# Top-k attention with a capacity-limited mixture of experts: a new order of VectorE's work inside a pipeline step, and one copy for q and k

## The chip, the cores and the metric

The kernel runs on one core of a Trainium2 chip. The metric is the device time of one execution in microseconds (us), the median of several runs. The core has five engines that matter here: TensorE (PE in the profile), VectorE (DVE), ScalarE (ACT), GpSimd (POOL) and SyncE (SP), which issues the DMA transfers. Matrix products land in PSUM, everything else is worked on in SBUF.

## The reference, cut to what matters

Attention over 8 batches, 8 heads, 576 tokens and a head size of 64. Of every row of 576 scores only the 32 largest are kept. A mixture-of-experts layer follows, with one expert for each token and at most 80 tokens for each expert.

```python
def _attn_ref(q, k, v):
    B, H, S, D = q.shape                                  # 8, 8, 576, 64
    top_k = 32
    scores = scale * np.matmul(q, k.transpose(0, 1, 3, 2))
    kth = np.partition(scores, -top_k, axis=-1)[..., -top_k:-top_k + 1]
    mask = scores >= kth
    scores = np.where(mask, scores, -1000000000.0)
    scores = scores - np.max(scores, axis=-1, keepdims=True)
    attn = np.exp(scores)
    attn = attn / (np.sum(attn, axis=-1, keepdims=True) + 1e-09)
    return np.matmul(attn, v).astype(np.float32)

# x = attention's result as (4608, 512); for each expert e of 8, at most 80 tokens:
#   out[tok] = gate_w[tok] * (relu(x[tok] @ w1[e]) @ w2[e])
```

The change is in the attention alone.

## The kernel before

The attention is a software pipeline written as a list of engine instructions in a fixed order. Its item of work is a **unit**: 128 rows (queries) of one head with their 576 scores. A pair of heads has nine units, numbered 0 to 8 here: four row blocks with two heads each (0 and 1, 2 and 3, 4 and 5, 6 and 7), and one last unit, 8, that holds the 64 rows left over from both heads. There are 32 head pairs, so 288 units. The second unit of each of the four blocks (1, 3, 5, 7) is in the set `odd`; unit 8 and unit 0 of the next pair are both not in it.

The threshold of a unit is found in these pieces, each of which is one letter in the step's schedule:

```python
def parts(self, i):                       # G: six of these, 96 scores each
    for j in range(NG):
        nc.vector.max(out=cand[:, j, :], in_=s[:, j * S // NG : (j + 1) * S // NG])
        yield

def search(self, i):
    for r in range(3):                    # a, c, e: a maximum over the 48 candidates
        nc.vector.max(out=dst, in_=cand)
        if r == 2:                        # after e: ScalarE compares and counts
            nc.scalar.activation(sign, s, Act.Sign, bias=w9[:, 7:8], scale=-1.0, accum_out=cnt)
        yield
        if r < 2:                         # b, d
            nc.vector.match_replace(out=cand, in_to_replace=dst, in_values=cand, imm_value=LOW)
            yield
    y = self.rows.tile([P, S], F32, name="y", tag="y", bufs=1)
    engine = nc.gpsimd if i in self.odd else nc.vector
    engine.tensor_tensor(out=y, in0=s, in1=sign, op=Alu.mult)      # y: the product
    yield
    nc.vector.max(out=w9[:, 8:], in_=y)                            # g: the search in the product
    yield
    nc.vector.scalar_tensor_tensor(out=pick, in0=past, scalar=cnt, in1=w9[:, 7:],
        accum_out=self.thr[:, i : i + 1], op0=Alu.is_equal, op1=Alu.mult)   # h: the pick
    yield

def below(self, i):                       # m: the mask
    if i in self.odd:
        nc.scalar.activation(self.mask[i], self.s[i], Act.Relu, bias=self.thr[:, i : i + 1], scale=-1.0)
        return
    engine = nc.vector if i == NU - 1 else nc.gpsimd
    engine.tensor_scalar(self.mask[i], self.s[i], self.thr[:, i : i + 1], None, op0=Alu.is_lt)
```

One call of `step(i, ...)` works on several units at once. The letters b to e belong to the unit one behind `i`, y to the unit two behind, g three behind, h and m four behind; G and a belong to `i` itself, and z is a small reciprocal.

```python
back = dict(a=0, b=1, c=1, d=1, e=1, y=2, g=3, h=4, m=4)
for c in "hmgyGbGcGdGGGeaz" if i - 2 in self.odd else "hmgGbGcGdGeGGyaz":
    ...                                   # the letter's next piece, for unit i - back[c]
if whole(i - 4): self.turn_w(...)         # TensorE: scores and mask turned and added, then ScalarE's exponential
...
if busy: self.front(...)                  # TensorE: scores of a later unit; ScalarE copies them out of PSUM
if whole(i - 5): self.back(...)           # TensorE: weights times v
if due and not busy: self.turn(due.pop()) # once for each head pair
```

`turn` turns q and k of the next head pair on TensorE and copies them out of PSUM on ScalarE:

```python
four = self.four()                                        # four PSUM banks
ps = [four[:, 2 * j : 2 * j + 2, :].rearrange("p j c -> p (j c)") for j in range(2)]
for j, src in enumerate(self.qk.pop(n)):
    self.turn_in(ps[j], src.rearrange("p c h d -> p c (h d)"))
self.turned[n] = [self.qkp.tile([P, S], F32, name=name, tag=name) for name in ("qT", "kT")]
for j in range(2):
    nc.scalar.copy(self.turned[n][j], ps[j][:, :S])
```

Each engine takes its instructions in the order in which the loop emits them, so the letters are VectorE's order, and, for y and m of the units that go there, GpSimd's.

Of the kernel before, what the change touches and what calls it, by code (L numbers as in the profile page):

```python
# [9 lines left out]
F32 = mybir.dt.float32  # L10
# [17 lines left out]
def kernel(  # L28
# [11 lines left out]
    nc = tc.nc  # L40
    B, H, S, D = q.shape
# [8 lines left out]
    P = 128  # L50
# [76 lines left out]
    class Attention:  # L127
# [53 lines left out]
        def turn(self, n):  # L181

            four = self.four()
            ps = [four[:, 2 * j : 2 * j + 2, :].rearrange("p j c -> p (j c)") for j in range(2)]
            for j, src in enumerate(self.qk.pop(n)):
                self.turn_in(ps[j], src.rearrange("p c h d -> p c (h d)"))
            self.turned[n] = [self.qkp.tile([P, S], F32, name=name, tag=name) for name in ("qT", "kT")]
            for j in range(2):
                nc.scalar.copy(self.turned[n][j], ps[j][:, :S])

        def front(self, n, t):

# [199 lines left out]
        def run(self, slow):  # L392

            units = []
            for n in range(NP):
                for t in range(NF):
                    units += [(n, t, 0), (n, t, 1)]
                units.append((n, NF, 2))
            self.odd = {i for i, unit in enumerate(units) if unit[2] == 1}
            first, second = {}, {}  # L400
            later = []
            due = []
            drawn = []
            ready = {}

            def whole(i):

                return 0 <= i < NU and units[i][2] > 0

            def step(i, last):  # L410
                if 0 <= i < NU:
                    n, t, h = units[i]
                    if t == 2 and h == 1 and n + 2 < NP:
                        self.load(n + 2, *divmod(n + 2, HP))
                    if t in (1, 3) and h == 0 and slow and n:
                        slow.pop(0)()
                    if t == 0 and h == 0 and n + 1 < NP:
                        due.append(n + 1)
                    first[i] = self.parts(i)

                back = dict(a=0, b=1, c=1, d=1, e=1, y=2, g=3, h=4, m=4)

                for c in "hmgyGbGcGdGGGeaz" if i - 2 in self.odd else "hmgGbGcGdGeGGyaz":
                    if c == "G":
                        if 0 <= i < NU:
                            next(first[i])
                    elif c == "a":
                        if 0 <= i < NU:
                            next(first[i], None)
                            second[i] = self.search(i)  # L430
                            next(second[i])
                    elif c == "z":
                        for u in drawn:
                            self.over(*u)
                    elif c == "m":
                        if 0 <= i - back[c] < NU:
                            self.below(i - back[c])
                    elif i - back[c] in second:
                        next(second[i - back[c]])
                if whole(i - 4):  # L440
                    self.turn_w(*units[i - 4][:2])
                for u in drawn:
                    self.divide(*u)
                ends = [n for n, t in drawn if t == NF]
                drawn.clear()
                busy = 0 <= i + 4 < NU and units[i + 4][2] != 1
                if busy:
                    self.front(*units[i + 4][:2])
                if whole(i - 5):
                    self.back(*units[i - 5][:2])  # L450
                    drawn.append(units[i - 5][:2])
                if due and not busy:
                    self.turn(due.pop())
                    busy = True
                for g in list(later):
                    if ready[g] and busy and not last:
                        continue
                    busy = busy or ready[g] == 1
                    ready[g] = next(g, None)
                    if ready[g] is None:  # L460
                        later.remove(g)
                for n in ends:
                    b, hp = divmod(n, HP)
                    later.append(self.norm(n, b, hp, b % 2, 2))
                    ready[later[-1]] = 0

            with tc.manual_schedule():
                self.load(0, 0, 0)
                self.load(1, *divmod(1, HP))
                nc.sync.dma_start(wg, moe_w_gate.rearrange("(c p) e -> p c e", p=P))  # L470
                self.turn(0)
                i = -4
                while i < NU + 6 or later:
                    step(i, i >= NU + 6)
                    i += 1
            assert not slow and not due
# [410 lines left out]
```

## Time and profile before

The median time is 1022.78 us (three runs, 1022.1 to 1024.26). The profiled execution has a span of 1027.5 us. All 288 units lie in its first 890 us or so; the experts follow.

| line, engine | what it is | count | median or mean ns of one |
|---|---|---|---|
| L213 DVE | G, a maximum over 96 scores | 1728 | 244 |
| L224 DVE | a, c, e | 864 | 199 |
| L232 DVE | b, d (a load and a replace) | 576 | 191 |
| L236 DVE | y on VectorE | 160 | 740 |
| L236 POOL | y on GpSimd | 128 | 1281 |
| L238 DVE | g, the search in the product | 288 | 755 |
| L241 DVE | h, the pick | 288 | 211, mean 290 |
| L254 POOL | m on GpSimd | 159 | 1721 |
| L250 ACT | m on ScalarE | 128 | 777 |
| L229 ACT | sign and count | 288 | 777, and 198 for the count |
| L189 ACT | copies of q and of k | 32 each | 643 and 647 |

How to read it: durations of neighbours on VectorE overlap[...]. What an instruction costs its engine is the distance from its start to the next start, which the timeline shows: 0.16 us for a G of 0.24, 0.67 us for a g of 0.755.

### The profile page before, as it was taken

To read this page: it belongs to the slowest core of one execution; us is meant where nothing else is said; L and a number is where in the kernel's file an instruction comes from. 1 tells how busy PE (TensorE), PEld (TensorE's weight loads), DVE (VectorE), ACT (ScalarE), POOL (GpSimd) and SP (SyncE) were. 2 spreads that over 40 slices of the span, in tenths; PEclk is the share of its full clock that TensorE was granted. 3 is DMA by queue.
4 is the path that set the end of the run, shared out by engine and by line. 5 is a ranking of instruction groups with operands and counts; after the bars stand their busy time and mean duration, and the time that the engine had idled before them with its cause. 6 is when DMAs were issued, how large, how long until landed. Compare 5 with 4: busy or idle time off the path is not lost.

```text
span 1027.5 us, 35579 instructions
## 1 busy us (share of the span) xinstructions
PE 902.3 (88%) x13381; PEld 728.9 (71%) x13381; DVE 896.0 (87%) x5087; ACT 786.2 (77%) x1671; POOL 456.1 (44%) x331
## 2 busy tenths in 40 slices
PE   5889999999889999989899999998999998598896
PEld 3677777777667777777677777776777777588886
DVE  3999999999999999999999999999999999551000
ACT  3888899888888898888898888898888988401110
POOL 1444555554454545554454544555454554211101
PEclk9999999999999999999999999999999999879998
DMA  4344443333333323233333311111221200326800
GB/s 93 77 118 129 122 128 89 89 89 89 90 88 89 80 72 81 77 81 84 85 89 89 89 41 38 46 45 48 48 49 48 49 13 14 119 77 214 325 23 25
DMA packets 167893, 85.76 MB, mean 83 GB/s; under 512 B 117792, under 2 KB 154656, under 8 KB 167712
## 3 DMA queue, kind: packets, MB, share of 16 engines
q1 hardware_dynamic: 166688, 80.78, 28.4%
q0 software_dynamic: 1024, 2.62, 0.8%
q8 instruction: 107, 1.75, 0.7%
q14 instruction: 74, 0.61, 0.2%
HBM read 63.19 MB, written 20.19 MB: 81 GB/s over the span
## 4 chain that ended last, share of the span: by engine, by line
DVE 54%; PE 30%; ACT 11%; issue 2%; another core or an unknown queue 1%; DMA 0%; SPq 0%; POOL 0%; POOLq 0%; ACTq 0%; DVEq 0%
DVE cand L213 17%; DVE w L238 12%; PE cc L309 7%; DVE cand L232 6%; DVE y L236 6%; DVE pick L241 4%; DVE top L224 4%; PE yp L776 3%; PE sp L201 3%; PE ab L286 3%; ACT wT L295 3%; PE sp L178 2%; ACT sign L229 2%; PE warm L632 2%; DVE w L224 2%
## 5 line engine op out<-in xcount | busy, mean ns | idle before, releaser
L213 DVE MAX8 cand<-s 128x8 f32<-128x96 f32 x1728 | 387.0, 244 | 9.5 <-ACT s L206 9.5
L254 POOL TENSOR_SCALAR mask<-s,thr_all 128x576 bf16<-128x576 f32 x159 | 273.7, 1721 | 199.6 <-PE ab L291 130.6
L309 PEld LDWEIGHTS cc<-vb,wT 128*64 128x64 f32 x5760 | 201.2, 139 | 111.5 <-ACT wT L295 94.6
L236 POOL TENSOR_TENSOR y<-s,sign 128x576 f32<-128x576 f32 x128 | 164.0, 1281 | 240.3 <-ACT sign L229 104.2
L309 PE MATMUL cc<-vb,wT 128*64 128x65 f32 x5760 | 223.4, 225 | 52.1 <-ACT wT L295 52.1
L229 ACT ACTIVATE sign<-s,w 128x576 bf16<-128x576 f32 x288 | 226.0, 785 | 44.9 <-DVE w L224 44.5
L238 DVE MAX8 w<-y 128x8 f32<-128x576 f32 x288 | 217.4, 755 | 2.2 <-POOL y L236 2.0
L201 PE MATMUL sp<-kT,qT 64*128 64x288 f32 (+1 forms) x1280 | 202.0, 435 | 14.7 <-ACT part L353 6.1
L286 PE MATMUL ab<-ident,s 128*128 128x128 f32 x1152 | 176.5, 282 | 10.9 <-ACT wT L295 10.9
L206 ACT ACTIVATE s<-sp 128x1152 f32<-128x1152 f32 (+1 forms) x160 | 167.2, 1045 | 11.4 <-PE sp L201 9.8
L286 PEld LDWEIGHTS ab<-ident,s 128*128 128x128 f32 x1152 | 128.3, 142 | 34.6 <-ACT wT L295 25.1
L295 ACT ACTIVATE wT<-ab 128x1024 f32<-128x1024 f32 (+1 forms) x160 | 150.8, 942 | 0.0
L201 PEld LDWEIGHTS sp<-kT,qT 64*128 64x128 f32 (+1 forms) x1280 | 105.5, 179 | 53.4 <-ACT part L353 8.0
L236 DVE TENSOR_TENSOR y<-s,sign 128x576 f32<-128x576 f32 x160 | 118.2, 739 | 3.1 <-ACT sign L229 2.6
L224 DVE MAX8 top<-cand 128x8 f32<-128x48 f32 x576 | 114.4, 199 | 0.1
L291 PEld LDWEIGHTS <-mask 128*128 128x128 bf16 x1440 | 94.5, 98 | 25.8 <-ACT mask L250 19.0
L232 DVE MATCH_REPLACE8 cand<-top,cand 128x48 f32<-128x48 f32 x576 | 110.0, 191 | 0.0
L250 ACT ACTIVATE mask<-s,thr_all 128x576 bf16<-128x576 f32 x128 | 99.5, 777 | 0.4 <-DVE pick L241 0.4
L330 ACT ACTIVATE xn<-cc,z_all 128x64 f32<-128x64 f32 (+1 forms) x320 | 82.8, 316 | 2.3 <-DVE z_all L321 2.3
L241 DVE SCALAR_TENSOR_TENSOR pick<-past,cnt,w 128x9 f32<-128x9 f32 x288 | 83.6, 290 | 0.0
L286 PE MATMUL cc<-ident,s 128*128 128x128 f32 x288 | 79.0, 274 | 0.2 <-ACT xn L330 0.2
L293 ACT ACTIVATE wT<-cc 128x256 f32<-128x256 f32 (+1 forms) x160 | 57.5, 359 | 6.0 <-PE cc L291 4.4
(192 smaller groups left out, 981.5 us busy)
## 6 DMA issues: line engine op xcount, KB each, us to landing
w<-in_moe_w_dram SPq DMA_DIRECT2D x32, 512.0 KB, 4.3
w<-in_moe_w_dram SPq DMA_DIRECT2D x8, 2048.0 KB, 12.6
out_dram<-zero SPq DMA_DIRECT2D x9, 1024.0 KB, 5.9
qn<-in_q_dram SPq DMA_DIRECT2D x64, 128.0 KB, 2.4
kn<-in_k_dram SPq DMA_DIRECT2D x64, 128.0 KB, 2.5
vb<-in_v_dram SPq DMA_DIRECT2D x64, 128.0 KB, 2.5
xd<-xn SPq DMA_DIRECT2D x32, 256.0 KB, 4.1
qn<-in_q_dram SPq DMA_DIRECT2D x32, 32.0 KB, 2.3
```

The costliest lines, as they stand in the source:

```text
L201: nc.tensor.matmul(o, lhsT=qT[d, t * P : t * P + m], rhs=kT[d, j * HS : (j + 1) * HS], start=True, stop=True)
L206: nc.scalar.activation(s[:, : g * S].rearrange("p (j c) -> p j c", c=HS), ps[:, : 2 * g, :HS], Act.Copy, scale=TINY)
L213: nc.vector.max(out=cand[:, j, :], in_=s[:, j * S // NG : (j + 1) * S // NG])
L224: nc.vector.max(out=dst, in_=cand)
L229: nc.scalar.activation(sign, s, Act.Sign, bias=w9[:, 7:8], scale=-1.0, accum_out=cnt)
L232: nc.vector.match_replace(out=cand, in_to_replace=dst, in_values=cand, imm_value=LOW)
L236: engine.tensor_tensor(out=y, in0=s, in1=sign, op=Alu.mult)
L238: nc.vector.max(out=w9[:, 8:], in_=y)
L254: engine.tensor_scalar(self.mask[i], self.s[i], self.thr[:, i : i + 1], None, op0=Alu.is_lt)
L286: nc.tensor.matmul(dst[h][c], lhsT=sc[:, keys[c]], rhs=ident, start=c == 0 or (c == NF and h == 0), stop=False, is_transpose=True, skip_gr ...
L295: nc.scalar.activation(wT[:, : g * NF, :], ab.rearrange("p h c r -> p (h c) r")[:, : g * NF, :], Act.Exp, scale=scale / TINY)
L309: nc.tensor.matmul(cc[r : r + TL, o], lhsT=wT[:, j * NF + c if c < NF else 2 * NF + j, r0 : r0 + TL], rhs=vb[:, c, h, :], start=(c == 0), ...
```

## The change

Two things are changed. In steps in which g reads a product that GpSimd made (`i - 3` in `odd`), two part maxima and one replacement (G b G) are placed ahead of the pick, its mask and the search, so that GpSimd has longer to finish. In all other steps the search g is placed ahead of the pick h and the mask m, and the product y, where it goes to GpSimd, behind G b G. And q and k leave PSUM in one ScalarE operation over both instead of two.

```diff
@@ turn
-            self.turned[n] = [self.qkp.tile([P, S], F32, name=name, tag=name) for name in ("qT", "kT")]
-            for j in range(2):
-                nc.scalar.copy(self.turned[n][j], ps[j][:, :S])
+            both = self.qkp.tile([P, 2, S], F32, name="both", tag="both")
+            nc.scalar.copy(both, four.rearrange("p (k j) c -> p k (j c)", k=2)[:, :, :S])
+            self.turned[n] = both[:, 0, :], both[:, 1, :]
@@ step
-                for c in "hmgyGbGcGdGGGeaz" if i - 2 in self.odd else "hmgGbGcGdGeGGyaz":
+                head = "GbGhmg" if i - 3 in self.odd else "ghmGbG"
+                for c in head + ("ycGdGGGea" if i - 2 in self.odd else "cGdGeGGya") + "z":
```

## The prediction

> **What bounds the kernel now.** I read the busy shares first, then the same shares for the steady part alone, then the longest waits, then the pick's own line, and last one round of nine units in order of time. The page's first part and the stretch from 50 to 800 us:
>
> ```profile
> PE 902.3 (88%) x13381; PEld 728.9 (71%) x13381; DVE 896.0 (87%) x5087; ACT 786.2 (77%) x1671; POOL 456.1 (44%) x331
> ```
>
> ```profile
> 50.00:800.00 750.00, 675.77 (x9582) 537.70 (x9582) 749.34 (x4341) 670.28 (x1425) 382.85 (x252) 1.00 0.30 79
> ```
>
> In the second line the third busy time is VectorE's: 749.34 of 750 us. It looks saturated, and if that were true a change that only reorders its instructions could gain nothing. But the pick's line, asked for by its source, does not look like work of one size:
>
> ```profile
> L241 DVE SCALAR_TENSOR_TENSOR pick<-past,cnt,w x288: 168/211/1003, 23.2 to 880.9; 128x9 f32<-128x9 f32 x144
> ```
>
> Nine elements take 211 ns in the median and up to 1003. The timeline of one round, VectorE first, shows what the long ones are (columns: start in us, duration, engine, line, operation):
>
> ```profile
> 534.60 0.20 DVE L241 SCALAR_TENSOR_TENSOR pick<-past,cnt,w 128x9 f32<-128x9 f32 x1
> 534.73 0.08 DVE L241 DVE_READ_ACCUMULATOR pick<-past,cnt,w 128x1 f32 x1
> 534.73 0.75 DVE L238 MAX8 w<-y 128x8 f32<-128x576 f32 x1
> 535.40 0.24 DVE L213 MAX8 cand<-s 128x8 f32<-128x96 f32 x1
> ...
> 536.94 0.21 DVE L224 MAX8 top<-cand 128x8 f32<-128x48 f32 x1
> 537.07 0.93 DVE L241 SCALAR_TENSOR_TENSOR pick<-past,cnt,w 128x9 f32<-128x9 f32 x1
> 537.92 0.08 DVE L241 DVE_READ_ACCUMULATOR pick<-past,cnt,w 128x1 f32 x1
> 538.00 0.76 DVE L238 MAX8 w<-y 128x8 f32<-128x576 f32 x1
> ```
>
> GpSimd in the same round:
>
> ```profile
> 535.00 1.72 POOL L254 TENSOR_SCALAR mask<-s,thr_all 128x576 bf16<-128x576 f32 x1 [4.60 <-PE ab L291]
> 536.69 1.28 POOL L236 TENSOR_TENSOR y<-s,sign 128x576 f32<-128x576 f32 x1
> ```
>
> The second pick stretches until 538.00, and GpSimd's product ends at 537.97. So the search of unit 1 waits for GpSimd's product, and the wait is hidden in the record of the pick ahead of it. Without a wait, pick to search is 0.13 us (534.60 to 534.73); here it is 0.93, so 0.80 us is waiting. Going through the 32 rounds, the pick of unit 0 takes 0.93 to 0.94 us to the next start in 30 of them (1.01 in one and 2.26 in the first), and nearly every other pick takes 0.13 to 0.15. The one other place is the pick of unit 4, ahead of the search of unit 5: about 0.08 us over in seven rounds, 0.33 and 0.47 in two. A round is 26.74 us between its searches, so VectorE really works 25.94 of them.
>
> What holds GpSimd? ScalarE's sign for the unit, or GpSimd's own earlier work:
>
> ```profile
> 534.55 0.79 ACT L250 ACTIVATE mask<-s,thr_all 128x576 bf16<-128x576 f32 x1
> 535.23 0.77 ACT L229 ACTIVATE sign<-s,w 128x576 bf16<-128x576 f32 x1
> 535.89 0.20 ACT L229 ACTIVATION_READ_ACCUMULATOR sign<-s,w 128x1 f32 x1
> ```
>
> The sign and its count are done at 536.09; the product starts at 536.69, 0.60 us later, and that is when the mask in front of it on GpSimd ends (535.00 + 1.72 = 536.72). So this is the mask of unit 8, which, with unit 0 behind it, is the one place where a mask and a product fall to GpSimd in the same step. The chain, from the step's start at 534.60: pick of unit 8 (its count is read out at 534.81), mask 0.19 us later, 1.72 of mask, 1.28 of product, search at 538.00. That is 3.40 us, and VectorE has 2.60 us of work beside it. In nearly all rounds the product starts within 0.05 us of the mask's end and 0.6 us after the sign.
>
> **What the Trainium skill says.** "PSUM — Partial Sum Buffer", section "Engine vs sequencer instructions", has the queues of ScalarE, VectorE and GpSimd strictly first in, first out. The trace agrees: the product's inputs are complete at 536.09 and it stands behind the mask until 536.69. "Perfetto Trace Analysis", section "DVE / Act Engine Instruction", places the wait for semaphores ahead of the recorded window. Here the wait of one instruction lengthens the record of the one before it (0.20 to 0.93 us), so the measurement decides and the 749.34 us are not all work. The same page, "Optimizing Scalar/DVE Operations", gives ScalarE about 51 ns of fixed cost for an operation on PSUM and advises grouping. The trace allows the same estimate: the two copies take 1.07 us from start to start (533.48 and 534.55 for what follows them), and ScalarE's other copy of 1152 elements out of PSUM, the scores, 1.01 (530.60 to 531.61).
>
> **The change part by part.** (1) *G b G ahead of the pick behind a GpSimd product.* From the timeline, G, b and the next G take 535.40 to 535.90, 0.49 us from start to start. The search of unit 1 is reached 0.49 us later in its step, and the rest of that step is shorter by as much. Alone this would cut the wait from 0.80 to 0.31. It would also end the small waits at unit 5: 7 x 0.08 + 0.33 + 0.47 = 1.4 us in the whole kernel.
>
> (2) *The search ahead of the pick elsewhere.* The step with unit 0's search is such a step, since 0 isn't odd, and its pick is that of unit 8. The search comes first, 0.67 us from start to start (534.73 to 535.40), then the pick. VectorE's sum is the same, but the pick that starts GpSimd's chain is now 0.67 us later: mask 535.67 to 537.39, product 537.36 to 538.64, search of unit 1 at 538.67 instead of 538.00. The letter m still stands ahead of y, so GpSimd keeps its order.
>
> Both together: from the step's start to the search of unit 1 the chain takes 3.40 + 0.67 = 4.07 us. VectorE's own work up to it is 2.60 + 0.49 = 3.09. The wait becomes 0.98. The search comes 0.67 later, and what follows is shorter by 0.49: **+0.18 us a round**, in 31 rounds +5.6 us. In the first round there is no mask of an earlier unit 8 and the wait is for the sign; there G b G saves 0.5.
>
> (3) *Moving y behind G b G* changes nothing on VectorE: it's a GpSimd instruction there, and it waits for the mask in its own queue.
>
> (4) *One copy for q and k.* 0.06 us of ScalarE a round, estimated above. It brings the sign of unit 1 forward by as much, and the sign is 0.60 us early already. Worth 0 on the path.
>
> (5) *Later masks elsewhere.* GpSimd's other masks come up to 0.49 us later. TensorE uses them 2.2 us or more after their end, that of unit 8 mostly 1.2 us, at least 1.0. ScalarE's masks of units 1 and 3 start about 0.9 us after their picks now. They lose 0.67 and still 0.18 by the longer wait, so 0.05 us is left: tight, but ScalarE also waits 44.5 us in all for VectorE ahead of its signs, and catches up there.
>
> Sum: +5.6 - 0.5 - 1.4 = **+3.7 us**, so 1022.8 + 3.7 = about 1026 us.
>
> **Rivals.** *The wait shrinks as the change intends.* If mask 8 were held by something other than its pick, the chain would not move and 31 x 0.49 = 15 us would be gained, 1007 us. For it: ScalarE's turn of q and k falls into the same stretch, and the waits' view names the sign as the product's releaser (104.2 us in 38 waits). Against it: the mask starts a constant 0.19 us after the pick's read-out, in every round, and the product right at the mask's end. *ScalarE becomes the bound.* Its masks and signs slip behind the later picks, TensorE gets the mask late (it waits for ScalarE's mask in every round already), and 0.2 us more a round makes 1033. For it: ScalarE is busy 670 of 750 us and its slack at the masks shrinks to nearly nothing. Against it: after each mask comes a sign that waits for VectorE anyway. *The order is a wash,* if VectorE issues the new neighbours more tightly or the copy counts for more than I think: 1020 to 1024.
>
> **Range and chances.** The step per round rests on durations that repeat to 0.01 us, so +3.7 is good to perhaps 3 us either way if the chain is right; the tail on the slow side is ScalarE, on the fast side the wait that shrinks. 8 in 10: 1018 to 1032. For over 2% faster all 28 us of hidden waiting would have to go (to below 1002.3): 0.03. For over 2% slower something not seen here: 0.02.
>
> **What would show it.** In the changed kernel the pick stands ahead of unit 1's search as before and should take about 1.11 us to it once a round (0.98 of wait); the mask of unit 8 should start 0.19 us after its pick, some 1.07 us after the step's start; the round should be 26.9 us. If the wait has fallen to 0.3 and the round to 26.3, step (2) is wrong. If the wait is right and the round longer than 27, it is ScalarE. If the product starts behind the sign and not behind the mask, the chain that I name is not the one.

## The result and the profile after

The changed kernel takes 1028.14 us in the median (1026.56 to 1029.3), the kernel before 1022.52 us measured beside it (1022.1 to 1024.26). The ratio is 1.0051, with a 95% interval of 1.0032 to 1.0069: slower by 0.3 to 0.7%, or 3.3 to 7.1 us. The prediction was 1026 us, +3.7 us.

The spans of the two profiled executions don't show this difference, since both are 1027.5 us. The profiled execution of the kernel before was, with 1029.23 us, slower than the others of it, and what follows its last search g is 147.0 us long against 142.2 after. The part that was changed does show it: from the first search g to the last, 858.9 us before and 863.9 after, 5.0 more.

The page's first part and the stretch from 50 to 800 us of the kernel after look like those of before (the columns are those of the prediction's lines; VectorE is the third busy time of the second):

```profile
PE 900.5 (88%) x13381; PEld 727.3 (71%) x13381; DVE 900.6 (88%) x5087; ACT 780.5 (76%) x1639; POOL 456.7 (44%) x331
```

```profile
50.00:800.00 750.00, 671.86 (x9540) 534.44 (x9536) 749.35 (x4308) 660.85 (x1386) 380.32 (x250) 1.00 0.31 79
```

VectorE is "busy" for 749.35 of 750 us again, but it began 4308 instructions in that time where it began 4341 before. Nearly the same busy time and less work done: either its instructions take longer, or a wait is recorded as work. The pick's line points to a wait (168/211/1003 before):

```profile
L241 DVE SCALAR_TENSOR_TENSOR pick<-past,cnt,w x288: 201/213/1103, 23.4 to 886.7; 128x9 f32<-128x9 f32 x144
```

Before, the longest pick of a typical round was 0.93 us; now it is 1.1. The same place of a round in order of time, VectorE:

```profile
563.62 0.74 DVE L238 MAX8 w<-y 128x8 f32<-128x576 f32 x1
564.27 0.21 DVE L241 SCALAR_TENSOR_TENSOR pick<-past,cnt,w 128x9 f32<-128x9 f32 x1
564.41 0.08 DVE L241 DVE_READ_ACCUMULATOR pick<-past,cnt,w 128x1 f32 x1
...
566.42 0.25 DVE L213 MAX8 cand<-s 128x8 f32<-128x96 f32 x1
566.59 1.09 DVE L241 SCALAR_TENSOR_TENSOR pick<-past,cnt,w 128x9 f32<-128x9 f32 x1
567.61 0.07 DVE L241 DVE_READ_ACCUMULATOR pick<-past,cnt,w 128x1 f32 x1
567.69 0.76 DVE L238 MAX8 w<-y 128x8 f32<-128x576 f32 x1
```

GpSimd and ScalarE in the same stretch:

```profile
564.68 1.72 POOL L254 TENSOR_SCALAR mask<-s,thr_all 128x576 bf16<-128x576 f32 x1 [4.78 <-DVE cand L213]
566.37 1.28 POOL L236 TENSOR_TENSOR y<-s,sign 128x576 f32<-128x576 f32 x1
```

```profile
562.50 1.13 ACT L188 COPY both<-sp 128x1152 f32<-128x1152 f32 x1 [0.99 <-PE sp L179]
563.51 0.78 ACT L250 ACTIVATE mask<-s,thr_all 128x576 bf16<-128x576 f32 x1
564.19 0.76 ACT L229 ACTIVATE sign<-s,w 128x576 bf16<-128x576 f32 x1
564.86 0.19 ACT L229 ACTIVATION_READ_ACCUMULATOR sign<-s,w 128x1 f32 x1
```

The step starts at 563.62 with the search of unit 0. The pick of unit 8 comes 0.65 us later, the mask of unit 8 starts 0.19 after the pick's read-out (564.49 to 564.68), the product follows at the mask's end, and the search of unit 1 at 567.69, 4.07 us after the step's start. The sign was done at 565.05, 1.32 us before the product could start. The bracket behind the mask's line is the profile's guess at what the mask waited for; it can mislead. In the kernel before it named TensorE's work with an earlier mask (PE ab L291), a rival to the pick. That work ended 0.04 us ahead of the mask in most rounds before, but 0.71 us ahead of it now, while the distance from the pick's read-out to the mask is 0.19 us in every round of both (0.20 in one): the pick is what the mask waits for.

Through the rounds the pick of unit 0 takes 1.10 to 1.11 us to the next start in every round but the first, and the round between searches of unit 0 is 26.95 us in the median, 26.74 before.

### The profile page after: what moved, and what is told of

Same layout as the page of the kernel before. It is cut to its first block, busy times and chain, and to the rows that moved or that the text cites. A ratio compares the mean times of both kernels' runs of the same rounds, so it can differ in the third digit from the quotient of the medians.

```text
span 1027.5 us, 35545 instructions
## 1 busy us (share of the span) xinstructions
PE 900.5 (88%) x13381; PEld 727.3 (71%) x13381; DVE 900.6 (88%) x5087; ACT 780.5 (76%) x1639; POOL 456.7 (44%) x331
## 3 DMA queue, kind: packets, MB, share of 16 engines
q0 software_dynamic: 1024, 2.62, 0.8%
## 4 chain that ended last, share of the span: by engine, by line
DVE 84%; PE 12%; ACT 2%; issue 1%; DMA 0%; SPq 0%; POOL 0%; POOLq 0%; DVEq 0%; ACTq 0%
DVE cand L213 26%; DVE w L238 19%; DVE y L236 10%; DVE cand L232 10%; DVE pick L241 6%; DVE top L224 6%; PE yp L777 4%; DVE w L224 3%; DVE z_all L321 2%; PE cc L309 1%; PE sp L201 1%; PE warm L633 1%; PE acc L702 1%; DVE mg L672 1%; DVE top L670 1%
## 5 line engine op out<-in xcount | busy, mean ns | idle before, releaser
L201 PE MATMUL sp<-both 64*128 64x288 f32 (+1 forms) x1280 | 202.1, 435 | 14.6 <-ACT part L353 6.1
L201 PEld LDWEIGHTS sp<-both 64*128 64x128 f32 (+1 forms) x1280 | 105.6, 179 | 53.3 <-ACT part L353 8.0
L291 PEld LDWEIGHTS <-mask 128*128 128x128 bf16 x1440 | 94.5, 98 | 27.3 <-ACT mask L250 19.5
L241 DVE SCALAR_TENSOR_TENSOR pick<-past,cnt,w 128x9 f32<-128x9 f32 x288 | 88.3, 307 | 0.0
L188 ACT COPY both<-sp 128x1152 f32<-128x1152 f32 x32 | 36.1, 1127 | 36.3 <-PE sp L179 36.3
```

The lines of the kernel that those rows point to most:

```text
L201: nc.tensor.matmul(o, lhsT=qT[d, t * P : t * P + m], rhs=kT[d, j * HS : (j + 1) * HS], start=True, stop=True)
```

## The experiments

The theory: the pick of unit 8 behind unit 0's search makes GpSimd's mask late, and the product of unit 1 stands behind that mask in GpSimd's queue. Rivals: the merged copy costs; VectorE's new order costs by itself, in all steps; ScalarE sets the pace. Each run is given against the kernel before as it was measured beside it: 1028.91 us beside the first four runs, 1022.74 beside the next four, 1022.96 beside the last two. So ratios and differences compare from run to run, and times do not.

### The merged copy alone

```diff
 the kernel before; the lines that allocate the tiles are left out
-            for j in range(2):
-                nc.scalar.copy(self.turned[n][j], ps[j][:, :S])
+            nc.scalar.copy(both, four.rearrange("p (k j) c -> p k (j c)", k=2)[:, :, :S])
```

> The kernel before with only the copy of q and k merged. The theory (the pick of unit 8 behind unit 0's search sends GpSimd's mask, and with it the product of unit 1, late) says that the copy is off the path: the sign of unit 1 comes 0.06 us earlier and still waits behind the mask, pick to search of unit 1 stays 0.93 us, a round 26.74 us, the time within 1 us of before. The rival 'the merged copy costs' (it holds four PSUM banks until its end) says 4 to 6 us more. The rival 'ScalarE sets the pace' says 2 us less.

Measured: 1027.82 us, ratio 0.9993 (0.9983 to 1.0003). The round is 26.74 us. VectorE around the search of unit 1:

```profile
562.74 0.93 DVE L241 SCALAR_TENSOR_TENSOR pick<-past,cnt,w 128x9 f32<-128x9 f32 x1
563.60 0.08 DVE L241 DVE_READ_ACCUMULATOR pick<-past,cnt,w 128x1 f32 x1
563.67 0.76 DVE L238 MAX8 w<-y 128x8 f32<-128x576 f32 x1
```

The wait is what it was. The sign is done 0.66 us ahead of the product instead of 0.60, so the copy did save its 0.06 us, where nothing waited for it.

### The new order alone

```diff
 the kernel before
-                for c in "hmgyGbGcGdGGGeaz" if i - 2 in self.odd else "hmgGbGcGdGeGGyaz":
+                head = "GbGhmg" if i - 3 in self.odd else "ghmGbG"
+                for c in head + ("ycGdGGGea" if i - 2 in self.odd else "cGdGeGGya") + "z":
```

> The kernel before with only the new order of letters. The theory says all of the change is here: pick to search of unit 1 1.10 us, a round 26.94 us, 4 to 6 us more than before. The rival 'the merged copy costs' says no more than before or less.

Measured: 1033.96 us, ratio 1.0056 (1.0039 to 1.0074), pick to search 1.10 us, a round of 26.95. Its pick's line:

```profile
L241 DVE SCALAR_TENSOR_TENSOR pick<-past,cnt,w x288: 200/212/1104, 23.7 to 885.7; 128x9 f32<-128x9 f32 x144
```

That is 5.0 us more, where the whole change lost 5.6: the loss is in the order.

### Half of the order: pick and mask first where the product was VectorE's

```diff
 the run before
-                head = "GbGhmg" if i - 3 in self.odd else "ghmGbG"
+                head = "GbGhmg" if i - 3 in self.odd else "hmgGbG"
```

> Half of the new order: G b G ahead of pick, mask and search where the search reads a GpSimd product; everywhere else pick and mask ahead of the search as in the kernel before (y still behind G b G). The theory says that the chain from the pick of unit 8 is again 3.40 us while VectorE has 3.09 us of work beside it: pick to search of unit 1 0.44 us, a round 26.25 us, 15 to 17 us less than before (1006 to 1008). The rival 'ScalarE sets the pace' (its signs fall behind when VectorE hurries) says at most 5 us less, with waits at other searches. The rival 'new neighbours cost VectorE' says no gain.

Measured: 1013.13 us, ratio 0.9847 (0.9827 to 0.9867), 15.8 us less than before. A round is 26.24 us. VectorE, then GpSimd, around the search of unit 1:

```profile
551.06 0.21 DVE L241 SCALAR_TENSOR_TENSOR pick<-past,cnt,w 128x9 f32<-128x9 f32 x1
...
554.03 0.43 DVE L241 SCALAR_TENSOR_TENSOR pick<-past,cnt,w 128x9 f32<-128x9 f32 x1
554.39 0.08 DVE L241 DVE_READ_ACCUMULATOR pick<-past,cnt,w 128x1 f32 x1
554.47 0.76 DVE L238 MAX8 w<-y 128x8 f32<-128x576 f32 x1
```

```profile
551.47 1.72 POOL L254 TENSOR_SCALAR mask<-s,thr_all 128x576 bf16<-128x576 f32 x1 [4.11 <-PE ab L291]
553.16 1.28 POOL L236 TENSOR_TENSOR y<-s,sign 128x576 f32<-128x576 f32 x1
```

From the step's start (551.06) the chain takes 3.41 us again, as before, and VectorE has 2.97 us to the pick of unit 0, 0.50 more than before. So 0.44 us is left from pick to search, of which 0.30 is waiting. This part of the change does what it was meant to do, and saves the 15 us that the prediction gave it.

### The changed kernel with one step of nine put back

```diff
 the changed kernel
-                head = "GbGhmg" if i - 3 in self.odd else "ghmGbG"
+                head = "GbGhmg" if i - 3 in self.odd else "hmgGbG" if (i - 3) % UPP == 0 else "ghmGbG"
```

> The changed kernel, with the old order (pick, mask, then search) restored in one step of nine alone, the one whose pick is of unit 8. The theory says that this one step is the whole loss: the same as with the old order restored in all of them, a round 26.25 us, 15 to 17 us less than before. If the loss were spread over all the steps with the search first (ScalarE's masks that come later behind their picks), only a ninth to a fifth of it would come back and the time would stay above before.

Measured: 1012.2 us, ratio 0.9845 (0.9824 to 0.9867), the same as the run before. Its pick's line:

```profile
L241 DVE SCALAR_TENSOR_TENSOR pick<-past,cnt,w x288: 200/212/444, 23.6 to 866.6; 128x9 f32<-128x9 f32 x144
```

No pick's record is longer than 0.44 us, though the search still comes first in the four other steps of a round. The loss is that one step's. A round is 26.28 us here against 26.24, so the search ahead of the pick costs 0.04 to 0.05 us in those four steps together.

### GpSimd's queue turned round in the kernel before

```diff
 the kernel before
+                odd_turn = "hgymGbGcGdGGGeaz" if (i - 4) % UPP == UPP - 1 else "hmgyGbGcGdGGGeaz"
-                for c in "hmgyGbGcGdGGGeaz" if i - 2 in self.odd else "hmgGbGcGdGeGGyaz":
+                for c in odd_turn if i - 2 in self.odd else "hmgGbGcGdGeGGyaz":
```

> The kernel before with one thing changed, on GpSimd alone: in the step whose pick is of unit 8, the product of unit 1 is issued ahead of the mask of unit 8. VectorE's order is that of before. The theory (the product waits for the mask in GpSimd's queue) says that it starts right behind its sign, 0.6 us earlier than before: pick to search of unit 1 0.40 us, and a round up to 0.5 us shorter. The mask of unit 8 then ends 1.2 us later than TensorE wants it, which may give some of it back. The rival 'the sign or VectorE holds the product' says no earlier product.

Measured: 1059.3 us, ratio 1.036 (1.0346 to 1.0374). GpSimd, VectorE and TensorE in one round:

```profile
557.83 1.28 POOL L236 TENSOR_TENSOR y<-s,sign 128x576 f32<-128x576 f32 x1 [5.82 <-DVE top L224]
559.09 3.42 POOL L254 TENSOR_SCALAR mask<-s,thr_all 128x576 bf16<-128x576 f32 x2
```

```profile
558.68 0.45 DVE L241 SCALAR_TENSOR_TENSOR pick<-past,cnt,w 128x9 f32<-128x9 f32 x1
559.06 0.08 DVE L241 DVE_READ_ACCUMULATOR pick<-past,cnt,w 128x1 f32 x1
559.14 0.76 DVE L238 MAX8 w<-y 128x8 f32<-128x576 f32 x1
```

```profile
560.86 0.23 PE L291 MATMUL cc<-minus,mask 128*128 128x128 bf16 x1 [1.16 <-POOL mask L254]
```

```profile
562.68 0.17 DVE L321 RECIPROCAL z_all<-cc 128x2 f32<-128x2 f32 x1 [0.43 <-PE cc L309]
563.44 0.20 DVE L356 TENSOR_TENSOR lg<-lg,part 128x40 f32<-128x40 f32 x1 [0.59 <-ACT part L353]
```

The product starts 0.13 us after its sign (557.70), and pick to search falls from 0.93 to 0.46 us (0.40 was expected): the mask ahead of it in the queue had held the product beyond its sign. But the mask is now the one that comes late. TensorE stands idle for 1.16 us for it, and VectorE then loses, from start to start, 0.50 us ahead of the reciprocal, which waits for TensorE, 0.69 ahead of the sum of the logits (the experts' scores, L356), which waits for ScalarE's copy of them, and 0.52 at the search of unit 5. A round takes 28.06 us. The expectation allowed for giving some of the gain back, not for 36.6 us of loss.

### A longer head, for unit 1 and then for all odd units

```diff
 the third run
-                head = "GbGhmg" if i - 3 in self.odd else "hmgGbG"
+                head = "hmgGbG"
+                if i - 3 in self.odd:
+                    head = "GbGcGdhmg" if (i - 3) % UPP == 1 else "GbGhmg"
 (the letters that moved ahead are left out of the rest of that step)
```

> The kernel before with G b G ahead of the pick in steps behind a GpSimd product, as in the third run, and in the step with unit 1's search a longer head: G b G c G d, then pick, mask and search. The theory says that VectorE then has 3.09 + 0.44 = 3.53 us of work beside a chain of 3.40, so the wait at unit 1 is gone (pick to search 0.14 us). If nothing else binds, a round is 25.93 us and the time 25 us less than before. But the third run left only 0.02 us of slack at the search of unit 5, whose product is bound by ScalarE's sign; if ScalarE's chain up to there does not move with VectorE, 0.3 us comes back as a wait at unit 5 and the time stays 15 to 17 us under before.

Measured: 1005.58 us, ratio 0.9834 (0.9821 to 0.9848). That is 17.2 us less, where 25 were hoped for. Pick to search of unit 1 is 0.14 us: that wait is gone. Yet the round is 26.23 us, as in the third run, so 0.3 us came back elsewhere. It isn't at unit 5, where the expectation had looked for it (0.14 to 0.17 us). Next, the longer head in every step behind a GpSimd product.

> The same longer head in every step behind a GpSimd product. The theory says no wait at unit 1 and none at unit 5, a round of 25.93 us, 24 to 27 us less than before. If ScalarE sets the pace now, waits at the searches or at VectorE's own products come back and the time is that of the run before or more.

Measured: 1006.01 us, ratio 0.9846 (0.9832 to 0.9859), a round of 26.20. Past the first round no pick waits any more, at unit 5 either, and still 25.93 isn't reached, nor the 24 to 27 us (16.7 less). Taken apart from start to start, the round is 0.27 us longer than that of the run below that fills ScalarE's gap: 0.11 at VectorE's own product of unit 2 and 0.16 at the sum of the logits behind it. So waits came back elsewhere on VectorE, as the expectation's second case has it. The last run of these adds the merged copy.

> As the run before, with q and k copied by one operation. The theory says within 1 us of the run before; if ScalarE has become the bound, 1 to 2 us less.

Measured: 1004.28 us, ratio 0.9819 (0.9806 to 0.9832), a round of 26.14, 0.07 us less. The copy that was worth nothing in the kernel before is now worth what it saves, and all of it at the product of unit 2, so ScalarE is on the path. Its lines and VectorE's of one round:

```profile
548.16 1.13 ACT L188 COPY both<-sp 128x1152 f32<-128x1152 f32 x1 [0.99 <-PE sp L179]
...
553.18 0.81 ACT L229 ACTIVATE sign<-s,w 128x576 bf16<-128x576 f32 x1
553.85 0.23 ACT L229 ACTIVATION_READ_ACCUMULATOR sign<-s,w 128x1 f32 x1
...
554.89 0.19 ACT L353 COPY part<-sp 128x40 f32<-128x40 f32 x1 [0.16 <-PE sp L347]
```

```profile
554.11 0.76 DVE L236 TENSOR_TENSOR y<-s,sign 128x576 f32<-128x576 f32 x1
...
554.91 0.15 DVE L321 RECIPROCAL z_all<-cc 128x2 f32<-128x2 f32 x1
555.12 0.20 DVE L356 TENSOR_TENSOR lg<-lg,part 128x40 f32<-128x40 f32 x1
```

VectorE's own product of unit 2 starts 0.03 us after ScalarE's sign for it; in the kernel before it started 0.76 us behind in most rounds, 0.29 at the least. ScalarE's stretch up to that sign has no gap but the one of 0.99 us, in which it waits for TensorE's turned q and k. Still, little is lost at the product now (0.04 us). The larger wait is at the sum of the logits, which starts 0.21 us after the reciprocal instead of 0.07: it waits for ScalarE's copy of them, and that copy for TensorE. Whether ScalarE's gap is behind this too, these lines don't decide; the next run does.

### ScalarE's gap filled

```diff
 turn(): the copy is returned as a function instead of being issued there
 step(), behind self.below(...), the mask (m):
+                        while drawn_in:
+                            drawn_in.pop()()      # the copy of q and k
```

> The run with the longer heads and the one copy, and in it ScalarE's copy of q and k issued behind the mask that follows it, instead of ahead: the mask fills the 0.99 us in which ScalarE waits for TensorE's turned q and k. With the heads, VectorE's waits had moved from the search of unit 1 to ScalarE: its product of unit 2 waits for ScalarE's sign (0.03 us after it in every round), and the logits' sum for ScalarE's copy. If ScalarE binds there, it gains 0.69 us a round, and VectorE's own work is the bound: a round 25.93 to 25.98 us instead of 26.14, 5 to 6.5 us less than the run before, 23 to 26 us less than the kernel before. If TensorE is behind it, no gain.

Measured: 996.88 us, ratio 0.9745 (0.9728 to 0.9763), 26 us less than before; a round is 25.93 us. ScalarE, and VectorE at the search of unit 1:

```profile
542.80 0.80 ACT L254 ACTIVATE mask<-s,thr_all 128x576 bf16<-128x576 f32 x1
543.91 1.13 ACT L190 COPY both<-sp 128x1152 f32<-128x1152 f32 x1 [0.32 <-PE sp L179]
544.93 0.78 ACT L233 ACTIVATE sign<-s,w 128x576 bf16<-128x576 f32 x1
```

```profile
548.43 0.22 DVE L245 SCALAR_TENSOR_TENSOR pick<-past,cnt,w 128x9 f32<-128x9 f32 x1
548.58 0.08 DVE L245 DVE_READ_ACCUMULATOR pick<-past,cnt,w 128x1 f32 x1
548.58 0.75 DVE L242 MAX8 w<-y 128x8 f32<-128x576 f32 x1
```

The gap shrinks from 0.99 to 0.32 us, both waits of the run before are gone, and the round is the 25.94 us that the prediction had worked out as VectorE's own work. The run before stood 18.5 us under the kernel before, this one 26.1: 7.6 us gained, where 5 to 6.5 were expected. 0.20 us in each of 31 rounds makes 6.2 of them, and where the rest comes from is not shown.

The same move alone in the kernel before:

> The kernel before with that one move alone (both copies behind the mask). The theory says that in the kernel before ScalarE's sign is 0.6 us ahead of GpSimd anyway: pick to search of unit 1 stays 0.93 us, a round 26.74, and at most the small waits at unit 5 go, 0 to 1.5 us less. If ScalarE did bind the kernel before, 10 to 20 us less.

Measured: 1022.13 us, ratio 0.9993 (0.9984 to 1.0003), a round of 26.74. ScalarE's sign, GpSimd, and VectorE's pick:

```profile
559.83 0.79 ACT L233 ACTIVATE sign<-s,w 128x576 bf16<-128x576 f32 x1
...
559.87 0.21 DVE L245 SCALAR_TENSOR_TENSOR pick<-past,cnt,w 128x9 f32<-128x9 f32 x1
...
560.28 1.72 POOL L258 TENSOR_SCALAR mask<-s,thr_all 128x576 bf16<-128x576 f32 x1 [4.60 <-PE ab L295]
...
561.97 1.28 POOL L240 TENSOR_TENSOR y<-s,sign 128x576 f32<-128x576 f32 x1
562.34 0.93 DVE L245 SCALAR_TENSOR_TENSOR pick<-past,cnt,w 128x9 f32<-128x9 f32 x1
```

The sign is done 1.27 us ahead of the product instead of 0.60 (560.70 and 561.97), and the pick still takes 0.93; only the small waits at unit 5 are gone. ScalarE did not bind the kernel before. The same move is worth 0.8 us or nothing there and about 7.6 us once GpSimd's chain is out of the way.

## Why the prediction was right

**The chain.** Predicted 4.07 us from the step's start to the search of unit 1, mask 0.19 us behind the pick, wait 0.98: measured 4.07, 0.19, and about 0.97 (1.10 to 1.11, less the 0.14 of a pick without a wait). That the pick of unit 8 and no other part makes the loss is shown by putting back that one step, which turned a ratio of 1.0051 into one of 0.9845; that GpSimd's queue order is the link, by turning it round.

**The gain of G b G.** Predicted 0.49 us for each round alone, 15 us. The third run gave 0.50 and 15.8. The waits at unit 5 went, as predicted, and the first round's wait fell from 2.26 to 1.70 us from pick to search, 0.56 for the 0.5 that was predicted.

**The copy.** Predicted 0.06 us off the path and worth 0: measured 0.06 and a ratio whose interval holds 1.

**Later masks on ScalarE.** Predicted for units 1 and 3 to start 0.05 us after their picks: measured 0.07 to 0.08 in most rounds. No effect is seen: the parts that make up the longer round, below, hold no wait for ScalarE.

**The sum.** +3.7 predicted, +5.6 measured, with an interval from +3.3 to +7.1 that holds both. So small a total could be met by luck; the account rests on the rounds. The term that was mis-sized is the step per round, +0.18: it measured +0.204 (26.945 less 26.741). Taken apart from start to start, the picks with their wait grew by 0.17 us a round, the part maxima by 0.06 (8.83 instead of 8.77), and the searches shrank by 0.02: the five part maxima of a round that now stand between a pick and a replacement take 0.173 us to the next start instead of 0.159. The prediction had taken VectorE's sum as unchanged by the order. With the measured step its sum would be 6.3 - 0.5 - 1.4 = +4.4 us. The two traces differ by 5.0 from the first search g to the last. What is left to the measured 5.6 isn't told apart from the spread of the runs.

**The rivals.** "The wait shrinks as the change intends" fell: it would have needed a mask that doesn't hang on its pick. "The order is a wash" fell too: every execution took longer than its 1020 to 1024 us. "ScalarE becomes the bound" was wrong for this change and right for the next one: once VectorE no longer waits for GpSimd's chain, the move of one ScalarE copy takes 0.20 us off the round.

## What to carry to other kernels

Before moving an instruction back on a saturated engine, look at who waits for it: VectorE's own sum was nearly the same here (0.04 us a round more), but a small pick started a chain of 3.2 us on another engine, and only in the one step of nine where two items of GpSimd's work met. Look for waits inside the records of cheap instructions whose duration varies, since the busy share may not show them. And an improvement that is worth nothing now may be worth its full size once the wait in front of it is gone, so try it again then.

## What the runs showed of the hardware that was not expected

VectorE's wait for GpSimd's product is recorded, in every round but the first, in the pick ahead of the search: a pick of nine elements ran from 0.21 to 1.10 us as the product came later, while the search's own record stayed at 0.73 to 0.77 us. The engine's busy share stayed at 749.3 to 749.4 of 750 us whether it waited 0.8 or 0.97 us a round. But the same wait can be recorded as idle time. In the first round of the kernel before it is:

```profile
23.17 0.21 DVE L241 SCALAR_TENSOR_TENSOR pick<-past,cnt,w 128x9 f32<-128x9 f32 x1
23.30 0.08 DVE L241 DVE_READ_ACCUMULATOR pick<-past,cnt,w 128x1 f32 x1
25.42 0.76 DVE L238 MAX8 w<-y 128x8 f32<-128x576 f32 x1 [2.04 <-POOL y L236]
```

What decides between the two, no run here shows; the distance from start to start holds the wait in both. And order has a price of its own on VectorE: the same part maximum ahead of a replacement took 0.159 us to the next start, or 0.173 right behind a pick.
